# Six instead of three of the 28 products of a unit in an inner seven-product form, with every engine's order taken from a table: pooled attention and a snake-activated two-layer network on one Trainium2 core

## The chip, the cores and the metric

The kernel runs on one core of a Trainium2 chip. The metric is the device time of one execution in microseconds. The kernel before took 906.76 us (median of three runs, 905.39 to 907.78).

The engines are named as in the profile: PE (TensorE matmul) and PEld (its weight loads), DVE (VectorE), ACT (ScalarE), POOL (GpSimd), SP (SyncE, which issues most DMAs). Each works through its own list of instructions in order and waits on semaphores for the others.

## The reference

All tensors are float32. Attention runs over 8 batches of 8 heads with 576 queries of 64 dimensions; keys and values are first averaged over groups of 8 rows, so each head has 72 of them. The result, as 4608 tokens of 512, goes through a network of two matrices with a "snake" activation.

```python
k_p = k.reshape(B, H, Sp, 8, D).mean(axis=3)
v_p = v.reshape(B, H, Sp, 8, D).mean(axis=3)
scores = scale * np.matmul(q, k_p.transpose(0, 1, 3, 2))
attn = softmax(scores)                     # over the 72 keys
x = np.matmul(attn, v_p)                   # 4608 tokens x 512
h = x @ w_in                               # 512 x 2048
g = h + np.sin(alpha * h) ** 2 / (alpha + 1e-9)
out = g @ w_out                            # 2048 x 512
```

## The kernel before

**Units.** The 4608 tokens are cut into nine units of 512. A unit u has the hidden layer of its tokens (`hidden`, L806) and carries, between its matmuls, the attention of batch u + 1 (`carry`, L1154, puts each piece of it into one of 28 slots). Ahead of unit 0 stands `first_batch`, which loads everything, pools the first batch and computes its attention. Units 7 and 8 carry no attention; at the end of unit 8 the second layer begins (`outputs`), which goes on alone to the end. The hidden activations g travel through DRAM (`g_bridge`) between the two layers.

**Products.** Both layers use Strassen's algorithm in Winograd's form: a product of 2 x 2 blocks is made of seven block products, numbered 1 to 7, of sums of blocks. In the hidden layer the blocks of w_in and their sums (`self.A`, `combine_w_in`, L675 on POOL) are the stationary operands, and the blocks of x and their sums (`sums_of_x`, L804 on DVE, in the tile `home3`, called bt) the moving ones. A unit has four groups J = 0 to 3, each with the seven products in the order 1, 5, 6, 2, 7, 3, 4, so 28 products in all. A product is four matmuls of 128 x 128 by 256 columns (L834). A group holds four PSUM banks b1, b6, b5, b7; ACT copies a bank into the next one where both need the same partial sum (L810), and makes sines and squares (L984, L991); DVE makes the last additions (L809, L1036); the result g is stored (L1050).

**The inner form.** `inner_product` (L1002) splits one of the 28 products once more in the same way: seven matmuls of 128 columns (L1014) in place of four of 256. It is cut into four steps: `a` multiplies 1 and 5 into a bank of their own (7 or 6), and ACT copies both results, the first into two places of the product's bank (L1018) and the second into a small tile m (L1020); `b` multiplies 6 and 2, and ACT copies one quarter of the bank (L1024); `d` multiplies 7, and DVE adds m (L1029); `e` multiplies 3 and 4. The next step of the same product needs the copy or the addition of the step before, so other matmuls are put in between. In units 1 to 6 three of the 28 products have this form: product 5 in groups 2 and 3 and product 1 in group 3. Their sums of weights are made once, in unit 0, by `inner_w_in` (L769) on POOL (L794) in a tile of the q loads; their sums of x are made once a unit by `inner_x` (L782) on POOL (L794).

**Attention of a batch.** Keys and values are loaded (L121, L140, L145) and pooled by POOL (L131). PE turns the keys (L269), computes scores in two blocks (`two_scores`, L308, 32 and 40 matmuls); DVE takes the maximum and subtracts (L331, L332), ACT takes the exponential (L357, with a load of its table and another back to the sine's), DVE sums and inverts (L363, L364), POOL multiplies (L365), DVE turns blocks of 32 (L491 to L501) and 16 DMAs move them (L511); then `all_values` (L600, L613) multiplies with the values, and ACT writes x (L527). The q of a later batch is turned in the same way (L219, L224) and moved by 16 DMAs (L234).

**Order.** The order of instructions on each engine is that of the program's text: `hidden` writes the matmuls of its seven products by hand, with the extras of each slot between them and copies, sines, squares and additions placed one by one, partly a group late (`last_sines`, `finish_before`, `behind_order`). Tiles are taken from pools, and a tile's next use waits for all readers of the last.

Of the kernel before, what the change touches and what calls it, by code (L numbers as in the profile page):

```python
# [19 lines left out]
P = 128  # L20
POOL = 8
# [3 lines left out]

class Kernel:
    def __init__(self, tc, q, k, v, w_in, w_out, alpha, out):
        self.tc, self.nc = tc, tc.nc
# [12 lines left out]
        self.T = self.S // 4  # L56

        self.gd = self.nc.dram_tensor("g_bridge", (2, self.NJ * JW, P, self.B * self.S), F32, kind="Internal").ap()

    def home(self, i, shape):  # L60

        return (self.xp if i < 2 else self.xq).tile(shape, F32, name=f"home{i}")
# [15 lines left out]
    def q_tile(self, i):  # L78

        return self.qp.tile([P, 5 * self.H * self.D], F32, name=f"q{int(i)}")  # L80
# [35 lines left out]
    def load_k(self, b, e):  # L116
# [3 lines left out]
        t = self.kvp.tile([P, 2048], F32, name="kvin")[:NP * m, 0:3 * POOL * D]  # L120
        self.nc.sync.dma_start(out=t, in_=self.k[b, NP * e:NP * e + NP].rearrange("h (p x) d -> (h p) (x d)", x=3 * POOL))  # L121
        if b not in self.kp:
            self.kp[b] = self.ap.tile([NP * m, 3, 2, D], F32, name="kp")
# [9 lines left out]
    def load_v(self, b):  # L133

        nc, D, H = self.nc, self.D, self.H
        vm, vz = self.vp[b] = self.ap.tile([P, H // 2, D], F32, name="vm", bufs=2), self.ap.tile([P, H // 2, D], F32, name="vz", bufs=2)
        t = self.kvp.tile([P, 2048], F32, name="kvin")[:].rearrange("p (h x) -> p h x", h=4)
        x = self.kvp.tile([P, POOL * D], F32, name="vr", bufs=1)[:]
# [40 lines left out]
    def load_v_rows(self, b, main, rest):  # L179
# [6 lines left out]
        self.vp[b] = self.ap.tile([P, self.H // 2, self.D], F32, name="vm", bufs=2), self.ap.tile([P, self.H // 2, self.D], F32, name="vz", bufs=2)  # L186
# [19 lines left out]
    def turn_q(self, b, part):  # L206
# [8 lines left out]
        if part == 0:  # L215
            for e in range(2):
# [3 lines left out]
                if e == 0:  # L220
                    self.finish_before()
# [17 lines left out]
    def new_tr(self):  # L239
        return self.ap.tile([P, 20 * 5 * 32], F32, name="tr")[:]  # L240
# [8 lines left out]
    def attention(self, b):  # L249
# [44 lines left out]
        def two_scores(j):  # L294

            x = (self.turn + 1) % 5
# [22 lines left out]
        def shifts(i, m, ps):  # L319
# [6 lines left out]
            for z, o in zip(ps, y):  # L326
                w = list(z.shape)[:-1]
                mx = self.sm.tile([P, 12], F32, name="mx2")[:, 0:m * (1 + i % 2)]
# [15 lines left out]
        def shift(i, e, ps):  # L344

            n = rows[i]
            mx = self.sm.tile([P, NP], F32, name="mx")
# [11 lines left out]
        def norm(i):  # L359

            n = E(i).shape[1]
            sm = self.sm.tile([P, 12], F32, name="sm2")[:, 0:n]
# [4 lines left out]
        def new_a():  # L367
            self.aM = self.ap.tile([P, 4, 736], F32, name="aM")
# [71 lines left out]
        def norm_rest():  # L440

            n = 64
            sm = self.sm.tile([P, H], F32, name="sm")
# [146 lines left out]
        def all_values():  # L590
# [16 lines left out]
            nc.scalar.copy(out=self.sm.tile([P, 1], F32, name="order")[:], in_=rest[:, 1, 0:1])  # L607
# [7 lines left out]
            self.behind_order()  # L615
            self.behind_order = lambda: None
# [152 lines left out]
    def inner_w_in(self):  # L769

        w = self.q_tile(0)[:]
        at = 0
        for p, J0 in ((5, 2), (1, 3)):
            n = self.NJ - J0
            A = self.A[p][:].rearrange("p k (J j m) -> p k J j m", j=2, m=P)[:, :, J0:]
            L = lambda i, j: A[:, j, :, i]
            s1, s2, s3, s4 = (w[:, at + i * n * P:at + (i + 1) * n * P].rearrange("p (J m) -> p J m", m=P) for i in range(4))
            at += 4 * n * P
            self.sums(((s1, L(1, 0), L(1, 1), OP.add), (s2, s1, L(0, 0), OP.subtract), (s3, L(0, 0), L(1, 0), OP.subtract), (s4, L(0, 1), s2, OP.subtract)))
            self.W2[p] = J0, {1: L(0, 0), 2: L(0, 1), 3: s4, 4: L(1, 1), 5: s1, 6: s2, 7: s3}  # L780

    def inner_x(self, u):  # L782

        for p, x, out in ((5, self.bt[u][:, 0], self.last[:, 0:4 * P]),
                          (1, self.xT[u][:, 0:2, 0:TH], self.ex[:, 5].rearrange("p h x -> p (h x)")[:, 0:4 * P])):
# [20 lines left out]
    def hidden(self, u, extra):  # L806
# [4 lines left out]
        sin, square, early = self.sin, self.square, lambda G: G.J == (0 if G.u else 1)  # L811
        two = 0 < u < self.B - 1

        def begin(J):

            b1, b6, b5, b7 = (self.bank([P, JW, TH]) for _ in range(4))
            new = lambda n, **kw: self.hp.tile([P, 2, JW, 2, TH], F32, name=n, **kw)
            G = SimpleNamespace(u=u, J=J, b1=b1, b5=b5, b6=b6, b7=b7, g=new("h"), s=self.s,
                                p5=None, i1=None, i5=None, early=J == (0 if u else 1))
            if two and J > 1:  # L820
                G.i5 = self.inner_product(G, 5, b5, 7)
# [757 lines left out]
```

## Time and profile before

| what | value |
|---|---|
| three runs | 905.39, 906.76, 907.78 us |
| profiled execution: span from first to last instruction | 902.6 us (the trace gives no other time for it; the median lies 4.2 us above) |
| granted clock of TensorE | 1.000 |
| busy: POOL, DMA traffic | 210.5 us; 141.13 MB, 156 GB/s in the mean |
| first batch | 0 to 20 us, PE busy 20.0 |
| unit 0 | 20 to 86.45 us |
| units 1 to 6 | 86.45 to 416.8 us, 55.0 to 55.15 us each |
| unit 7 and most of unit 8 | 416.8 to 513 us, PE without idle time |
| second layer | to the end; 56 steps of seven products |

How to read it: a matmul's row in the trace has a modelled end, and matmuls overlap in the array, so the time that one costs is the distance of its start from the next one's. Every float32 matmul stands in the trace as two records, so a plain product is 8 records and an inner one 14. A "busy" PE can still hide holes of up to some 0.15 us in front of a record. PEld loads the weights of the next matmul beside PE; a wait for a semaphore is often booked there.

### The profile page before, as it was taken

To read this page: it belongs to the slowest core of one execution; us is meant where nothing else is said; L and a number is where in the kernel's file an instruction comes from. 1 tells how busy PE (TensorE), PEld (TensorE's weight loads), DVE (VectorE), ACT (ScalarE), POOL (GpSimd) and SP (SyncE) were. 2 spreads that over 40 slices of the span, in tenths; PEclk is the share of its full clock that TensorE was granted. 3 is DMA by queue.
4 is the path that set the end of the run, shared out by engine and by line. 5 is a ranking of instruction groups with operands and counts; after the bars stand their busy time and mean duration, and the time that the engine had idled before them with its cause. 6 is when DMAs were issued, how large, how long until landed. Compare 5 with 4: busy or idle time off the path is not lost.

```text
span 902.6 us, 17941 instructions
## 1 busy us (share of the span) xinstructions
PE 895.0 (99%) x7014; PEld 815.8 (90%) x7014; DVE 677.4 (75%) x1011; ACT 448.3 (50%) x1070; POOL 210.5 (23%) x216
## 2 busy tenths in 40 slices
PE   8999999999999999999999999999999999999998
PEld 5787888888888888888888999999999999999997
DVE  7685766768577685764458799979798888889895
ACT  5696776877768778687976611111111111111111
POOL 4788552824438253430000000000000000000000
PEclk9999999999999999999999999999999999999999
DMA  9965867759586595648216346261618162534401
GB/s 261 245 200 158 220 163 202 196 167 251 139 213 186 177 230 143 176 146 293 93 72 227 102 141 199 59 194 38 224 27 230 33 197 67 172 92 127 137 15 40
DMA packets 128747, 141.13 MB, mean 156 GB/s; under 512 B 46920, under 2 KB 95704, under 8 KB 128664
## 3 DMA queue, kind: packets, MB, share of 16 engines
q1 hardware_dynamic: 125880, 137.88, 53.2%
q10 hardware_dynamic: 2784, 2.11, 0.9%
q8 instruction: 56, 0.92, 0.4%
q14 instruction: 27, 0.22, 0.1%
HBM read 75.37 MB, written 47.19 MB: 136 GB/s over the span
## 4 chain that ended last, share of the span: by engine, by line
PE 91%; DMA 3%; DVE 2%; POOL 2%; SPq 1%; issue 0%; ACT 0%; DVEq 0%; POOLq 0%
PE PS L834 42%; PE PS L1312 41%; PE PS L1014 3%; PE PS L308 2%; PE PS L600 2%; DMA a<-in_moe_w_in_dram 2%; DMA kvin<-in_v_dram 1%; SPq L669 1%; PE PS L613 1%; DVE x L1267 1%; DMA h<-in_k_dram 1%; POOL kvin L131 0%; POOL as L675 0%; DVE s L1267 0%; POOL ex L365 0%
## 5 line engine op out<-in xcount | busy, mean ns | idle before, releaser
L834 PE MATMUL PS<-home,a 128*128 128x256 f32 x1104 | 257.9, 381 | 0.7 <-ACT home L527 0.5
L834 PEld LDWEIGHTS PS<-home,a 128*128 128x128 f32 x1104 | 205.2, 190 | 34.1 <-issue 5.0
L834 PE MATMUL PS<-home,as 128*128 128x256 f32 x768 | 183.0, 382 | 0.0
L834 PEld LDWEIGHTS PS<-home,as 128*128 128x128 f32 x768 | 141.6, 190 | 19.8 <-ACT PS L810 1.2
L1312 PE MATMUL PS<-s,wb 128*128 128x144 f32 x896 | 119.1, 286 | 0.0
L1362 POOL TENSOR_TENSOR cc<-cc,cb 128x576 f32<-128x576 f32 x1 | 2.0, 1976 | 501.8 <-DVE cb L1267 501.8
L1312 PEld LDWEIGHTS PS<-s,wb 128*128 128x128 f32 x896 | 113.7, 190 | 0.1
L991 ACT ACTIVATE s<-s,c 128x256 f32<-128x256 f32 (+1 forms) x228 | 113.5, 564 | 0.0
L809 DVE TENSOR_TENSOR h<-PS,p 128x512 f32<-128x512 f32 x72 | 49.2, 683 | 64.2 <-PE PS L834 36.3
L131 POOL TENSOR_TENSOR kvin<-kvin 96x768 f32<-96x768 f32 (+3 forms) x42 | 71.6, 1705 | 69.5 <-DMA kvin<-in_v_dram 67.9
L1440 ACT COPY PS<-PS 128x144 f32<-128x144 f32 x56 | 14.7, 263 | 145.0 <-PE PS L1312 135.5
L984 ACT ACTIVATE s<-h,al 128x256 f32<-128x256 f32 x144 | 65.6, 510 | 39.4 <-DVE h L809 39.3
L1312 PE MATMUL PS<-r,wb 128*128 128x144 f32 x512 | 73.3, 286 | 0.3 <-DVE r L1267 0.3
L1312 PE MATMUL PS<-s,a 128*128 128x144 f32 x512 | 73.2, 286 | 0.0
L1036 DVE TENSOR_TENSOR h<-PS,s 128x512 f32<-128x512 f32 x36 | 24.7, 687 | 59.8 <-ACT s L991 59.8
L984 ACT ACTIVATE s<-PS,al 128x256 f32<-128x256 f32 x144 | 60.1, 470 | 18.6 <-PE PS L834 17.7
L1312 PEld LDWEIGHTS PS<-r,wb 128*128 128x128 f32 x512 | 67.1, 190 | 0.5 <-DVE r L1267 0.5
L1312 PEld LDWEIGHTS PS<-s,a 128*128 128x128 f32 x512 | 67.1, 190 | 0.0
L810 ACT COPY PS<-PS 128x512 f32<-128x512 f32 x72 | 41.5, 576 | 35.0 <-PE PS L834 30.4
L1460 ACT COPY PS<-PS 128x144 f32<-128x144 f32 x56 | 14.7, 263 | 88.1 <-PE PS L1312 88.1
L1312 PE MATMUL PS<-s,we 128*128 128x144 f32 x384 | 54.9, 286 | 0.0
L1312 PE MATMUL PS<-x,wb 128*128 128x144 f32 x384 | 54.9, 286 | 0.0
(215 smaller groups left out, 1407.7 us busy)
## 6 DMA issues: line engine op xcount, KB each, us to landing
g_bridge<-h SPq DMA_DIRECT2D x72, 512.0 KB
r<-g_bridge SPq DMA_DIRECT2D x31, 1152.0 KB
out_dram<-o SPq DMA_DIRECT2D x122, 72.0 KB
kvin<-in_k_dram SPq DMA_DIRECT2D x14, 576.0 KB
q<-in_q_dram SPq DMA_DIRECT2D x7, 1024.0 KB
kvin<-in_v_dram SPq DMA_DIRECT2D x14, 512.0 KB
aM<-tr SPq DMA_DIRECT2D x54, 92.0 KB
aM<-tr SPq DMA_DIRECT2D x54, 88.0 KB
```

Source lines behind the costliest of these rows:

```text
L131: self.nc.gpsimd.tensor_tensor(out=t[..., 0:w] if w > D else out, in0=t[..., 0:w], in1=t[..., w:2 * w], op=OP.add)
L308: nc.tensor.matmul(ps[e][r0 + r:r0 + r + q.shape[-1], h, :], q[s], kb[s, hp, :], start=True, stop=True)
L600: nc.tensor.matmul(o[r:r + 64], w, x, start=start and i < 2, stop=False, skip_group_check=True)
L809: add = lambda o, x, y: nc.vector.tensor_tensor(out=o, in0=x, in1=y, op=OP.add)
L810: copy = lambda o, x: nc.scalar.copy(out=o, in_=x)
L834: nc.tensor.matmul(ps[:, jj, :], self.A[p][:, kk, f * P:(f + 1) * P], x[:, kk, :], start=(start and n == 0), stop=(kk == 1), skip_group_ch ...
L984: self.nc.scalar.activation(out=G.s[:, i, jj, j, :], in_=src[:, jj], func=AF.Sin, scale=self.al[:, f:f + 1])
L991: self.nc.scalar.activation(out=x, in_=x, func=AF.Square, scale=self.c[:, f:f + 1])
L1014: nc.tensor.matmul(o, W[m][:, G.J - J0], X[m], start=start and n == 0, stop=True, skip_group_check=True)
L1036: add = lambda o, x, y: self.nc.vector.tensor_tensor(out=o, in0=x, in1=y, op=OP.add)
L1312: nc.tensor.matmul(out, W[:, J // 2, J % 2, :], A[:, J, :], start=(start and J == 0), stop=(J == self.NJ - 1), skip_group_check=True)
L1440: nc.scalar.copy(out=x1[:, 0, :], in_=x0[:, 1, :])
```

## The change

Three things change together.

1. In units 1 to 6 the groups J = 1, 2 and 3 have both product 1 and product 5 in the inner form: six of 28 products.
2. `hidden` is written anew. In those groups product 1 of the next group is made step by step between the matmuls of products 7, 3 and 4, and product 5 between those of 6 and 2. In group 0 of these units product 5 stands behind product 7, and the two score blocks stand in slot 1 and in the middle of product 2, where they stood in slots 3 and 5.
3. A class `Order` stands between the kernel and the engines. It records each instruction with the regions that it reads and writes, gives each a key (part, unit, label, number), sorts each engine's list by a place from the table `PLAN`, keeps PE in the order of the text, and then emits them all so that none comes ahead of what it depends on. Tiles of one name become one lasting tile (or a ring of two or three), so that a later use waits for the regions that it touches.

Beside that, `inner_w_in` makes 24 sums of 128 columns instead of eight (four of 256, four of 128), the x sums of product 1 get a tile of their own, two squares of half size are joined in groups that had them apart, and the loads of g for the second layer stand behind a step's work instead of ahead of it, in another order.

The core of the diff:

```diff
+    def flush(self):
+        self.edges()
+        lines = {e: [t for t in self.tasks if t.eng == e] for e in self.ENG.values()}
+        for e, x in lines.items():
+            for n, t in enumerate(x):
+                t.at = n if e == "PE" else t.unit * UNIT.get(t.key[0][0], 0) + self.plan.get(t.key, 0)
+            x.sort(key=lambda t: t.at)
...
+            x = min(ready, key=lambda x: (x[0].eng != "PE", x[0].at))
+            t = x.pop(0)
+            t.f(*t.a, **t.k)
...
-        for p, J0 in ((5, 2), (1, 3)):
...
+        for J in range(self.J0, self.NJ):
+            for p in (5, 1):
...
+            extras()
+            product(G, 6, G.b6, (0, 1))
+            if two:
+                G.i5.a()
+            product(G, 6, G.b6, (2, 3))
+            copy(G.b7[:], G.b6[:])
+            if two:
+                G.i5.b()
+            extras()
+            product(G, 2, G.b1, (0, 1))
+            if two:
+                G.i5.d()
+            if J == 0:
+                for f in extra["mid"]:
                     f()
+            product(G, 2, G.b1, (2, 3))
+            if two:
+                G.i5.e()
...
+            product(G, 7, G.b7, (0, 1))
+            if N and not late:
+                N.i1.a()
+            product(G, 7, G.b7, (2, 3))
+            if late:
+                N.i1.a()
+                product(G, 5, G.b5, start=True)
+                copy(G.p5[:], G.b5[:])
+            add(G.g[:, 1, :, 1], G.b7[:], G.p5[:])
+            self.sin(G, 1, 1, G.g[:, 1, :, 1])
+            extras()
+            if N:
+                N.i1.b()
+            product(G, 3, G.b6, (0, 1))
+            if N:
+                N.i1.d()
+            product(G, 3, G.b6, (2, 3))
...
+            if N:
+                N.i1.e()
+            product(G, 4, G.b7)
...
-                if n == 3 and u + 1 < self.B:
-                    self.load_g(u + 1, ("r11", "r12", "r22"))
-                if n == 5 and u + 1 < self.B:
-                    self.load_g(u + 1, ("r21",))
...
+            if st and u + 1 < self.B:
+                self.load_g(u + 1, {3: ("r11", "r22"), 4: ("r12",), 5: ("r21",)}.get(n, ()))
```

On the engines' lists this makes 72 matmuls of 256 columns fewer and 126 of 128 columns more on PE, 54 more copies of the inner form on ACT with 24 squares of 256 columns fewer and 12 of 512 more, 18 more additions on DVE, and 16 more operations on POOL. The number of DMAs is the same. In unit 0, POOL's list has one of the new weight sums in front of the sums of w_in's second group, nine more among the sums of keys and values, and the other 14 behind; SP's list has single loads and stores of several kinds in turn where it had them kind by kind.

## The prediction, made before the changed kernel ran

> **What bounds the kernel now.** I read the page's first two parts, then the busy times by stage, then TensorE's instructions in order of time, then the chain of work that ended last.
>
> ```profile
> PE 895.0 (99%) x7014; PEld 815.8 (90%) x7014; DVE 677.4 (75%) x1011; ACT 448.3 (50%) x1070; POOL 210.5 (23%) x216
> PEclk9999999999999999999999999999999999999999
> ```
>
> TensorE (PE) is busy for 99% of the span at its full granted clock, so time is won only by giving PE less to do or by closing the small holes that a "busy" row, whose ends are modelled, hides. By stage:
>
> ```profile
> 20.00:84.70 64.70, 64.48 (x531) 51.66 (x532) 42.74 (x75) 46.68 (x100) 54.45 (x54) 1.00 0.77 211
> ...
> 540.00:902.00 362.00, 358.31 (x2925) 358.09 (x2924) 306.59 (x409) 62.30 (x199) 1.98 (x1) 1.00 0.41 117
> ```
>
> Columns: stretch, its length, then busy time (and count) of PE, PEld, DVE, ACT, POOL, then clock, DMA share, GB/s. Unit 0 (first row) has GpSimd (POOL) busy for 54.45 of 64.70 us, more than anywhere else; units 1 to 6 (next row, one of them) keep ACT at three quarters; in the output stage only PE and DVE matter.
>
> ```profile
> 141.50:196.60 55.10, 55.10 (x447) 47.22 (x447) 38.17 (x63) 41.19 (x96) 25.56 (x25) 1.00 0.71 193
> ```
>
> What one record costs PE is the distance of starts, not the record's length:
>
> ```profile
> 118.48 2.76 PE L834 MATMUL PS<-home,a 128*128 128x256 f32 x12
> 121.08 0.38 PE L1014 MATMUL PS<-home,q 128*128 128x128 f32 x2
> 121.30 0.39 PE L1014 MATMUL PS<-last,as 128*128 128x128 f32 x2
> 121.52 1.03 PE L834 MATMUL PS<-home,a 128*128 128x256 f32 x4
> 122.39 0.38 PE L1014 MATMUL PS<-home,a 128*128 128x128 f32 x2
> ```
>
> Twelve 256-column records take 121.08 - 118.48 = 2.60 us, 0.216 each; four 128-column records take 121.52 - 121.08 = 0.44, 0.111 each. Every f32 matmul is two records. The last chain confirms that PE sets the end:
>
> ```profile
> 537.40 360.92 PE PS L1312 x2944
> ```
>
> From 537.40 to the end PE never waits (360.92 / 2944 = 0.1226 a record). Nothing is to be won there; one hole of about 0.5 us lies just before, at 535 to 537, behind a DVE sum of 2.48 us.
>
> **The change, part by part.**
>
> *Products.* In units 1 to 6, 25 of 28 products are plain (4 matmuls of 256 columns: 8 x 0.216 = 1.727 us) and 3 are in the inner form (7 matmuls of 128: 14 x 0.1115 = 1.561, a few ns more for the changes of shape). After the change 6 are inner; the built order agrees (72 matmuls of 256 columns fewer, 126 of 128 more). So 18 products win 1.727 - 1.57 = 0.16 each: -2.9 us. This is on PE, which sets the end, and is nearly sure.
> The Trainium skill (TensorE: Matmul & The Clock Gate, "Wait — 56ns, not 53.3ns?") says that a warm matmul takes its columns at 2.4 GHz plus a fixed 2.5 ns or so, a reason against splitting. By it, as an estimate, two f32 passes a record would give 215.8 ns, as the rows do, and 109.2 ns where the rows give 111; the step would be -3.5 instead of -2.9 us. The rows decide.
>
> *Holes in units 1 to 6.* The period is (416.8 - 86.45) / 6 = 55.06 us. By rows PE needs 43.2 (plain) + 4.7 (inner) + 2.8 (scores, L308) + 3.4 (values, L600 and L613) + 0.25 (keys, L269) = 54.3. So 0.75 us a unit are holes. About half is the restart after a change of shape and stays. The rest are waits: the first scores wait 0.38 us a unit for the DVE add that finishes the unit before (PEld L308 behind DVE L1036, 2.3 us in 6 times), and products wait for an ACT copy (PEld L834 behind ACT L810, 2.3 us in 12 times). The new order moves that add and gives each bank copy its place; bounds are 0 and -0.4 a unit. I take -0.17: -1.0 us in six units.
>
> *New hand-offs.* Each inner product adds two ACT copies after its first pair, one after its second and one DVE add before its last:
>
> ```profile
> L1018 ACT COPY PS<-PS 128x256 f32<-128x256 f32 x18 | 6.7, 375 | 5.0 <-DVE PS L1029 4.9
> L1020 ACT COPY m<-PS 128x128 f32<-128x128 f32 x18 | 5.0, 276 | 0.0
> L1024 ACT COPY PS<-PS 128x128 f32<-128x128 f32 x18 | 4.5, 250 | 11.9 <-PE PS L1014 11.9
> ```
>
> The last two numbers ahead of the idle time are busy us and mean ns. Three more products a unit: 3 x (375 + 276 + 250) = 2.7 us of ACT, less 0.6 for squares that are joined (24 of 510 ns fewer, 12 of 714 ns more, over six units): 41.2 becomes 43.3 of some 54.4 us. DVE gets 3 x 433 ns (L1029): 38.2 becomes 39.5. Both lie beside PE. What could reach PE is the wait: between the steps of an inner product the new code mostly puts two plain matmuls, 0.86 us. From the start of a pair's last record, cover is 0.11 + 0.86 = 0.97 us and need is 0.27 (the record) + 0.375 (the copy) = 0.65, or 0.70 with DVE's 433. If a sine of 0.47 to 0.51 us stands ahead on ACT, or an add of 0.68 on DVE, the step is 0.2 to 0.4 late. The rows above show such a spacing today (pairs at 121.08 and 122.39 with four records of 0.216 between) and no lateness. I take 0; the ends are 0 and 0.2 late for a third of the 108 hand-offs, +7 us.
>
> *The earlier scores.* The two score blocks move forward in the unit, with 2.6 us of PE between them instead of 3.65. DVE has to empty the first block in that: 4 operations of 0.45 and 2 of 0.75, 3.3 us, of which the first 0.4 lie beside the block itself and the second block's late banks give another 0.55. It just fits if DVE does nothing else, and the order of DVE holds those six together. Cost 0, at most 0.3 a unit. The 16 moves of q (0.63 us each on SP) end earlier with it in units 2 to 6; at the start of unit 1 they end about when the second block wants them: +0.3, bounds 0 and +1.5.
>
> *Unit 0 on GpSimd.* The weights of the inner form become 24 operations of 128 columns instead of 8 longer ones:
>
> ```profile
> L794 POOL TENSOR_TENSOR ex<-home,ex 128x128 f32<-128x128 f32 x12 | 11.4, 946 | 0.5
> L794 POOL TENSOR_TENSOR last<-home 128x128 f32<-128x128 f32 x12 | 10.7, 888 | 88.9 <-DVE home L804 88.9
> ...
> L794 POOL TENSOR_TENSOR ex<-home 128x128 f32<-128x128 f32 x12 | 5.4, 454 | 0.0
> ```
>
> That is 24 x 0.45 = 10.9 to 24 x 0.95 = 22.7 us for today's 5.2 (79.73 to 84.4 by time). Ten of them stand ahead of the last sums of k, whose reader on PE comes at 84.44. In the new order one weight sum stands in front of the combinations of w_in and writes where the first score block of unit 0 reads, which ends at 36.9 on PE; GpSimd is idle from 32.6 until then (4.3 us), where it works today. From 37.0 on I add the rows up: 12 combinations of 1.27 (15.2), norms 5.1, sums of v 5.2 + 2.1, of k 7.6, small ones 2.9, ten weight sums at 0.55 (5.5), some 2.0 between them: 45.6 us, to 82.6. PE's demands come at 77.2 (product 7 of the last group), 79.0 (values) and 84.4 (k): 1 to 2 us of margin by these means. I take +0.3, ends 0 and +5.
>
> *The rest.* Later loads of g (a product or two of 0.98 us later, needed 20 us on) and the new order of the output stage: PE waits for nothing there today, DVE at 85% has little room; 0, ends -0.5 (the hole at 535) and +1.
>
> Sum: -2.9 - 1.0 + 0.3 + 0.3 = -3.3 us. The profiled execution has a span of 902.6; the three timed runs have a median of 906.76 (905.39 to 907.78), 4.2 more, for what lies around the span and for its being a good run. The sum is a difference and goes on the median: **903.5 us**. About 0.3% (2.7 us) is what a measurement of this kernel can tell from no change, so the forecast lies just beyond it.
>
> **Rivals.**
> 1. *Hand-offs late.* ACT and DVE work in order at 79% and 73%; if 18 of the 108 hand-offs are 0.18 late, the gain of 3.3 is gone; with 36 the time is 903.5 + 6.5 = 910.0, with 15 it is 906.2. For it: the spacing is mostly 0.86 now, where two of today's three products have 1.7 to 3.5 us at their first step. Against it: today's tight one loses nothing, and in the built order the copies stand ahead of the second of each pair of sines. Chance 0.20.
> 2. *GpSimd sets unit 0 (slower).* Place: POOL between 37 and 84 us. Price: ten weight sums at 0.89 instead of 0.45 (+4.4), sums of k and v at their long ends (+2.4), less about 1.9 of margin: +4.9, of which 0.3 is in the sum: 908.1 us. It decides from 3.6 us of lateness, that is when the sums ahead of k take 51 us instead of 45.6. For it: one shape takes 454 and 946 ns here, short at 79.7 to 84.4 us, where DVE is busy 1.32 of 4.67 us, mostly long at 87.4 to 93.3, where it is busy 4.96 of 5.90. Against: the rows of k, v and norms, which are most of the sum, were taken beside that same DVE. Chance 0.20. The Trainium skill (SBUF — State Buffer, "Terms") says that DVE and GpSimd arbitrate for one port pair and the loser stands for the whole instruction; the two windows agree with it. By it, as an estimate with DVE busy for two thirds of unit 0, most of the ten sums would stand at the long end, and this rival would be about as likely as the forecast.
> 3. *Another form than told.* If fewer than 6 products were inner, each would give 0.16 x 6 = 0.96 us back (906.4 with none new); the built order speaks against it. Chance 0.03.
>
> **How the numbers follow.** Forecast 0.57, of which 0.50 lies under 904.0 and 0.07 above; rival 1: 0.14 within 0.3%, 0.06 slower; rival 2: 0.12 and 0.08; rival 3: 0.03 within. So faster 0.50, same 0.36, slower 0.14. The low end, 900.5, takes all holes' bounds (-2.4) and the hole at 535 (-0.5) with the 2.9, nothing lost at the start (901.0), and 0.5 for the spread of the runs; the high end, 907.9, reaches into both rivals.
>
> **What would show it.** Right: units 1 to 6 start 54.3 to 54.6 us apart, 0.111 us per 128-column record, score blocks without the wait for L1036, unit 1 starting at 86 to 87 us, output stage as long as before. Wrong: holes of 0.1 to 0.4 between inner steps that end with an ACT copy or a DVE add (rival 1), or PE waiting for POOL at 77 to 85 us and unit 1 starting after 89 (rival 2). A change of time in the output stage would refute the sum's last term.

## The result, and the profile after

The changed kernel takes **909.18 us** (median of six runs, 908.26 to 909.87) against 906.08 for the kernel before on the same chip (six runs, 905.11 to 907.78): ratio 1.0036, 95% interval 1.0025 to 1.0047. It is 3.1 us slower, where 2.6 us faster was forecast, and lies above the range (900.5 to 907.9). In the tables below "+" is slower.

The profiled execution has a span of 907.6 us; the one of the kernel before had 902.6. First the page's own first part and its clock line, then busy time by stage (stretch, its length, busy time and count of PE, PEld, DVE, ACT, POOL, clock, DMA share, GB/s), both of the changed kernel:

```profile
PE 894.9 (99%) x7122; PEld 813.5 (90%) x7122; DVE 661.0 (73%) x1029; ACT 458.2 (50%) x1112; POOL 199.0 (22%) x232
...
PEclk9999999999999999999999999999999999999999
```

```profile
22.40:88.90 66.50, 63.93 (x528) 51.28 (x529) 41.80 (x74) 45.96 (x95) 52.85 (x56) 1.00 0.68 183
144.20:199.10 54.90, 54.90 (x464) 46.97 (x463) 37.41 (x66) 42.42 (x103) 22.79 (x25) 1.00 0.68 193
545.00:907.00 362.00, 358.32 (x2926) 358.11 (x2924) 297.13 (x407) 63.87 (x199) 1.98 (x1) 1.00 0.41 116
```

PE's busy time is the same to 0.1 us with 108 records more, and the clock is full. Unit 0 (first row) has 2.6 us in which PE stands; before it had 0.2. The records themselves cost what was said: in the timeline of PE, four 256-column records take 190.12 - 189.25 = 0.87 us and four of 128 columns 189.25 - 188.81 = 0.44.

```profile
188.81 0.38 PE L156 MATMUL PS<-ex,q 128*128 128x128 f32 x2
189.03 0.39 PE L156 MATMUL PS<-home,as 128*128 128x128 f32 x2
189.25 1.03 PE L156 MATMUL PS<-home,a 128*128 128x256 f32 x4
190.12 0.41 PE L156 MATMUL PS<-ex,q 128*128 128x128 f32 x2
```

PE's waits in the changed kernel (engine, tile, line <- releaser: us in total, times, longest) are where to begin. All instructions that the class records show the line that emits them, L156, so one goes by tiles:

```profile
PE PS L156 <- DVE h L156: 2.1, 2, 1.2
PE PS L156 <- DMA q<-in_q_dram: 1.7, 1, 1.7
...
PE PS L156 <- POOL as L156: 0.9, 1, 0.9
...
PE PS L156 <- ACT PS L156: 0.5, 1, 0.5
```

The rest is bookkeeping by landmarks that both traces have: the first 256-column record (first product of unit 0), the turn of the keys (96x96) in each unit, the first and last 128x144 record of the second layer. From unit 1's end on the keys stand one product (1.73 us) later in the changed kernel's unit, which is taken out.

| stretch | before | after | difference |
|---|---|---|---|
| start to the first product of unit 0 | 19.98 | 22.38 | +2.40 |
| to the keys in unit 0 | 13.68 | 13.73 | +0.05 |
| to the keys at the end of unit 0 | 50.78 | 52.85 | +2.07 |
| unit 1 | 55.09 | 55.25 | +0.16 |
| units 2 to 5 | 220.44 | 219.63 | -0.81 |
| unit 6 to the end of unit 8 | 148.30 | 149.98 | +1.68 |
| output stage | 389.75 | 389.22 | -0.53 |
| its end | 4.61 | 4.60 | -0.01 |
| span | 902.63 | 907.64 | +5.01 |

A single profile is a weak witness at its start: this one began unit 0 at 22.4 us, where the six other profiles with the same start (experiments 2, 3, 4, 12 and the first ones of 9 and 10) begin it at 20.5 to 21.8. Units 1 on repeat to a few hundredths between profiles of the same code. Unit 0 takes 52.85 us wherever its code is that of the changed kernel, except once, 50.94 (experiment 12). The kernel before is no steadier there: its unit 0 took 50.78 in this profile and 50.22 in those of experiments 7 and 8, so the loss in unit 0 is 2.1 to 2.6 us. Outside the span there is another difference: time less span is 1.79 us in the runs of the kernel before and 2.25 in those of the changed one, +0.46.

### The profile page after: what moved, and what is told of

The parts are those of the page before. It is cut to its first block, busy times and chain, and to the rows that moved or that the text cites. A ratio compares the mean times of both kernels' runs of the same rounds, so it can differ in the third digit from the quotient of the medians.

```text
span 907.6 us, 18285 instructions
## 1 busy us (share of the span) xinstructions
PE 894.9 (99%) x7122; PEld 813.5 (90%) x7122; DVE 661.0 (73%) x1029; ACT 458.2 (50%) x1112; POOL 199.0 (22%) x232
## 4 chain that ended last, share of the span: by engine, by line
PE 95%; DMA 2%; ACT 1%; POOL 1%; DVE 1%; issue 0%; SPq 0%; DVEq 0%; POOLq 0%; ACTq 0%
PE PS L156 95%; DMA q<-in_q_dram 1%; ACT s L156 1%; POOL as L156 1%; DMA h<-in_k_dram 1%; DVE h L156 0%; SPq L156 0%; POOL a L156 0%; ACT L156 0%; ACT PS L156 0%; DVE mx L156 0%; DVE ex L156 0%; ACT ex L156 0%; DVE o L156 0%; DVE cc L156 0%
## 5 line engine op out<-in xcount | busy, mean ns | idle before, releaser
L156 ACT COPY PS<-PS 128x144 f32<-128x144 f32 (+4 forms) x312 | 115.8, 372 | 297.3 <-PE PS L156 285.4
L156 PE MATMUL PS<-home,a 128*128 128x256 f32 (+1 forms) x1080 | 252.0, 374 | 2.5 <-DVE h L156 2.1
L156 PEld LDWEIGHTS PS<-home,a 128*128 128x128 f32 x1080 | 195.6, 190 | 31.2 <-issue 4.5
L156 PE MATMUL PS<-home,as 128*128 128x256 f32 (+1 forms) x792 | 187.5, 372 | 1.4 <-POOL as L156 0.9
L156 PEld LDWEIGHTS PS<-home,as 128*128 128x128 f32 x792 | 143.0, 190 | 19.9 <-ACT PS L156 1.8
L156 PE MATMUL PS<-s,wb 128*128 128x144 f32 x896 | 119.1, 286 | 0.0
L156 ACT ACTIVATE s<-s,c 128x256 f32<-128x256 f32 (+1 forms) x216 | 117.6, 582 | 0.9 <-DVE h L156 0.7
L156 PEld LDWEIGHTS PS<-s,wb 128*128 128x128 f32 x896 | 113.7, 190 | 0.1
L156 POOL TENSOR_TENSOR cc<-cc,cb 128x576 f32<-128x576 f32 x1 | 2.0, 1978 | 498.5 <-DVE cb L156 498.5
L156 ACT ACTIVATE s<-h,al 128x256 f32<-128x256 f32 x144 | 70.8, 507 | 29.1 <-DVE h L156 28.7
L156 DVE TENSOR_TENSOR h<-PS,p 128x512 f32<-128x512 f32 x72 | 49.2, 684 | 47.8 <-PE PS L156 24.8
L156 POOL TENSOR_TENSOR kvin<-kvin 96x768 f32<-96x768 f32 (+3 forms) x42 | 69.9, 1665 | 41.3 <-DMA kvin<-in_k_dram 40.3
L156 ACT ACTIVATE s<-PS,al 128x256 f32<-128x256 f32 x144 | 63.8, 474 | 20.8 <-PE PS L156 20.4
L156 PE MATMUL PS<-r,wb 128*128 128x144 f32 x512 | 73.2, 286 | 0.0
L156 PE MATMUL PS<-s,a 128*128 128x144 f32 x512 | 73.2, 286 | 0.0
L156 DVE TENSOR_TENSOR h<-PS,s 128x512 f32<-128x512 f32 x72 | 48.8, 678 | 30.8 <-ACT s L156 30.8
L156 PEld LDWEIGHTS PS<-r,wb 128*128 128x128 f32 x512 | 67.1, 190 | 0.1
L156 PEld LDWEIGHTS PS<-s,a 128*128 128x128 f32 x512 | 67.0, 190 | 0.0
L156 POOL TENSOR_TENSOR ex<-ex,sm 128x576 f32<-128x576 f32 (+1 forms) x28 | 36.4, 1301 | 113.9 <-DVE sm L156 108.2
L156 PE MATMUL PS<-s,we 128*128 128x144 f32 x384 | 54.9, 286 | 0.0
L156 PE MATMUL PS<-x,wb 128*128 128x144 f32 x384 | 54.9, 286 | 0.0
L156 DVE TENSOR_TENSOR PS<-PS,m 128x256 f32<-128x256 f32 x36 | 15.6, 433 | 51.6 <-PE PS L156 49.4
```

The source lines that it names most:

```text
L156: t.f(*t.a, **t.k)
```

## The experiments

All ratios are to the kernel before, whose runs were taken on the same chip in the same series; 0.001 is 0.9 us. The table's lists are edited at one or two entries; `[27]` is entry 27 of a key.

**1. The start.** The trace's 1.7 us wait is for a load of q. SyncE issues it at 8.82 us, behind a load of w_in; before, it was issued at 6.99.

```profile
14.72 0.66 PE L156 MATMUL PS<-twos,home 128*128 128x64 f32 x4
17.09 0.66 PE L156 MATMUL PS<-ident,q 128*128 128x128 f32 x4 [1.71 <-DMA q<-in_q_dram]
```

```diff
-a.: ... [27] 391 [28] 477
+a.: ... [27] 298 [28] 300
```

> The changed kernel with one difference: SyncE issues the load of the q heads that the first turns of q need (the fourth load of q) and the second half load of v ahead of the first load of w_in, as the kernel before did. Theory A (places in the table lose the time): TensorE's wait of 1.7 us at 14.7 us for that load goes, everything behind it moves forward by as much; keys of unit 0 start at 34.4 instead of 36.1 us, and the time is 1.7 us under the changed kernel's 909.2, so +1.4 us or +0.15% over the kernel before. Rival B (the wait only moves): w_in then comes late, TensorE waits for it at 20 us, and the time stays at +3.1 us. Rival C (the start's loss was the spread of transfers in one run): the wait is gone or not by chance, time as the changed kernel's.

Measured: 1.0027 (1.0016 to 1.0039), 0.8 us better than the changed kernel; the wait is gone and unit 0 begins at 20.06. But ScalarE then waited for a later load of q and PE lost 0.9 us behind it before the keys. So the named wait went, as A said, and another came, though not the one for w_in that B named. The 0.8 by the clock is inside the intervals of the two ratios. Part of the 1.7 was C: the later kernels with this place unmended wait 0.4 to 1.5 us for that load and begin unit 0 at 20.5 to 21.8; those with it mended begin at 20.1 to 20.4. The means, with the changed kernel's own 22.4 among the late ones, differ by 1.0 us, which I take for what this place costs.

**2. The store at the end of unit 7.** A hole of 1.0 us at 479.4 us, by the distance of starts, ends with an addition into h. In the changed kernel:

```profile
479.91 0.69 DVE L156 TENSOR_TENSOR h<-PS,p 128x512 f32<-128x512 f32 x1 [1.73 <-PE PS L156]
...
480.64 0.91 ACT L156 ACTIVATE s<-h,al 128x256 f32<-128x256 f32 x2 [2.60 <-DVE h L156]
480.66 1.38 PEld L156 LDWEIGHTS PS<-home,a 128*128 128x128 f32 x7 [1.24 <-DVE h L156]
480.66 1.56 PE L156 MATMUL PS<-home,a 128*128 128x256 f32 x6 [0.84 <-DVE h L156]
```

The row of DVE names PE as its releaser. But the addition also waits for the store that reads its buffer, and SyncE's list shows that store late (changed kernel):

```profile
465.64 9.55 SPq L156 DMA_DIRECT2D g_bridge<-h  x4
475.29 5.09 SPq L156 DMA_DIRECT2D r<-g_bridge  x3
```

Four stores stand in one row, the first at 465.6 and the other three from 473.4. The table has one half of the first buffer's store behind both of the second's, which exist only at 473.4.

```diff
-7.: ... [158] 43592 [159] 43595 ... [210] 43594 [211] 43593
+7.: ... [158] 43592 [159] 43593 ... [210] 43595 [211] 43594
```

> The changed kernel with one difference: at the end of unit 7 SyncE issues both halves of the store of h's first buffer ahead of the two stores of its other buffer; the table had one half behind them, so that it waited for the last group of the unit. Theory A: the first addition of unit 8 into that buffer no longer waits for the late store (1.73 us of idle DVE), TensorE's hole of 1.0 us at 479.4 us goes, and the time is 1.0 us under the changed kernel's 909.2: +2.1 us over the kernel before. Rival B: the addition waits for TensorE, as the profile's row names it, and the hole of 1.0 stays: +3.1 us.

Measured: 1.0021 (1.0011 to 1.0031), 1.4 us better; unit 6 to the end of unit 8 takes 148.62 instead of 149.98. In this kernel's trace the same addition waits for nothing, so the named releaser was the wrong one and A holds:

```profile
475.13 1.28 DVE L156 TENSOR_TENSOR we<-wb,we 128x512 f32<-128x512 f32 x2
476.42 0.69 DVE L156 TENSOR_TENSOR h<-PS,p 128x512 f32<-128x512 f32 x1
```

**3. Unit 0, by its waits.** Two places were read off the trace; holes are given by the distance of starts, so that they are a little longer than the waits in brackets. PE stands 1.0 us at 47.7, put down to GpSimd; but I read that operand as GpSimd's sum that was done at 43.75, and ScalarE's bank copy, too, ended just before PE's start, in its list behind two sines, a copy and a square:

```profile
47.36 0.72 ACT L156 ACTIVATE s<-s,c 128x512 f32<-128x512 f32 x1
...
47.39 1.28 POOL L156 TENSOR_TENSOR as<-a,as 128x512 f32<-128x512 f32 x1
...
47.99 0.58 ACT L156 COPY PS<-PS 128x512 f32<-128x512 f32 x1
...
48.71 1.10 PE L156 MATMUL PS<-home,as 128*128 128x256 f32 x4 [0.89 <-POOL as L156]
```

And 1.4 us at 57 to 58.7, behind a DVE addition that took 3.38 us instead of 1.2 to 1.5 and made all of DVE's list late. It began 0.05 us behind one of GpSimd:

```profile
51.78 2.35 POOL L156 TENSOR_TENSOR kvin<-kvin 128x1024 f32<-128x1024 f32 x1
51.83 3.38 DVE L156 TENSOR_TENSOR h<-h,s 128x1024 f32<-128x1024 f32 x1
...
54.09 1.43 POOL L156 TENSOR_TENSOR q<-as 128x128 f32<-128x128 f32 x1
```

```diff
-0.: ... [49] 4148 ... [56] 2830 ... [80] 4155
+0.: ... [49] 4156 ... [56] 2227 ... [80] 4151.5
```

> The changed kernel with three places of unit 0 changed: ScalarE makes the bank copy for product 6 of group 1 ahead of two sines, a q copy and a square; VectorE adds product 5 (h<-PS,p) ahead of the sum of exponentials, and the addition over 1024 columns behind it. Theory A: the holes of 1.0 us (47.4) and 1.4 us (57.1 to 58.7) on TensorE go, and much of that at 64: -2 to -2.5 us, so +0.6 to +1.1 us over the kernel before. Rival B: VectorE meets GpSimd's long rows at another place, the 1024-column addition takes 3.4 instead of 1.3 us there too, and the lateness comes back before unit 1: +2.5 to +3.1 us.

Measured: 1.0037 (1.0023 to 1.0051), no gain by the clock. In the trace both holes are gone, and units 0 and 1 are 1.0 us shorter; a new hole of 1.2 us stands before the second score block, and the one near 64 us grew from 0.5 to 0.8. That settles the releaser of the first hole: here the same product starts at 46.36, behind the moved bank copy (done at 46.14), while GpSimd is still at the sums of 45.43 to 47.93. A on the two holes; B on the time but not by its path, since the addition over 1024 columns took 1.21 us at its new place: a mended wait let the next one through.

**4. The value products.** They take 3.82 us a unit instead of 3.42. A one-column copy that frees a bank for them stands behind a bank copy and a square on ScalarE (changed kernel):

```profile
192.92 0.19 PEld L156 LDWEIGHTS PS<-aM,vm 64*64 64x64 f32 x6 [0.24 <-ACT p L156]
...
193.15 0.62 ACT L156 COPY PS<-PS 128x512 f32<-128x512 f32 x1
...
193.66 0.19 ACT L156 COPY order<-PS 128x1 f32<-128x1 f32 x1
...
193.90 0.19 PEld L156 LDWEIGHTS PS<-aM,vm 64*64 64x64 f32 x4 [0.37 <-ACT order L156]
```

```diff
-u.all_values : ... [10] 8612
+u.all_values : ... [10] 8609.5
```

> The changed kernel with one place changed, in units 1 to 6 alike: ScalarE's one-column copy that the value products wait for stands directly behind the copy of product 5, ahead of a square and a bank copy. Theory A: the value products (3.82 us a unit in the changed kernel, 3.42 before) lose 0.2 to 0.35 us a unit, units 54.6 us apart instead of 54.9: -1.2 to -2.1 us, +1.0 to +1.9 us over the kernel before. Rival B: the bank copy that now comes 0.2 us later is what TensorE waits for next, and units stay 54.9 apart: +3.1 us.

Measured: 1.0031 (1.0019 to 1.0043); units 54.79 apart instead of 54.90. A in direction, but 0.11 us a unit where 0.2 to 0.35 were said: the other wait of this place, for the copy p, stayed. By the clock 0.5 us is not told from nothing.

**5. All of it, with the waits that followed.**

```diff
-0.load_v : ... [4] 1289      0.q_t : ... [19] 2849 [24] 2852
+0.load_v : ... [4] 1700      0.q_t : ... [19] 2235 [24] 2238
-0.: ... [108] 4436           u.: ... [216] 8609
+0.: ... [108] 4401           u.: ... [216] 8607.5
```

> The changed kernel with all four mended places together and the waits that came up behind three of them mended too: one load of v goes behind the q loads in the start (one run had ScalarE wait for that q), the q copies of unit 0 go ahead of a sine and two squares (the score block waited for them, 1.24 us), the bank copy of group 2 in unit 0 goes ahead of a sine and two squares (0.84 us), and in units 1 to 6 the copy of product 5 goes ahead of a sine (0.25 us a unit). Theory A (the places in the table lose the time, and each lost wait can be given its time back): from the changed kernel's +3.1 us, less 0.8 (start, as measured alone), 1.35 (store), 1.0 + 2.1 (unit 0), 0.7 + 0.6 to 1.5 (value products): -3.5 to -4.3 us under the kernel before, units 2 to 6 54.5 to 54.7 apart. Rival B (a wait that goes lets the next one through): only what the four gave alone, 0.8 + 1.35 + 1.0 + 0.7 = 3.85, -0.7 us.

Measured: 1.0005 (0.9996 to 1.0014), by 1.1 us worse than B, which gave 0.7 under the kernel before, and far from A. Start, store and value products keep their gains (units 54.74 apart), but unit 0 still takes 52.69: waits of 1.8 us before the score block, now behind a VectorE addition that waits for ScalarE's squares, and 0.9 behind 64.7. Two holes that move together when one is mended made me look for a cause further up the lists.

**6. No table at all.**

```diff
-                t.at = n if e == "PE" else t.unit * UNIT.get(t.key[0][0], 0) + self.plan.get(t.key, 0)
+                t.at = n
```

> The changed kernel with the table left out: every engine keeps the order of the text, with the same products on TensorE in the same order. Theory A (the table's misplaced entries are a few; most of it helps, since the text of the new form puts each bank copy behind the sines and squares of the group before): slower than the changed kernel by 5 us or more, with waits of 0.2 to 0.6 us on ScalarE copies in every group of units 1 to 6; period over 55.5 us. Rival B (ordering by the table is itself what loses): 903 to 906 us, period 54.3 to 54.6.

Measured: 1.246 (1.2401 to 1.2518), 1130 us; 87.4 to 88.8 us a unit. A, and far beyond its 5 us. Lines of this kernel's page and the two largest of PE's waits:

```profile
PE 983.4 (87%) x7122; PEld 863.4 (76%) x7122; DVE 679.1 (60%) x1029; ACT 463.1 (41%) x1112; POOL 203.3 (18%) x232
...
PEclk9989889898888888888988999999999999999999
```

```profile
PE PS L156 <- ACT PS L156: 95.4, 56, 3.4
PE PS L156 <- DVE ex L156: 29.9, 24, 2.8
```

The text of the new form is no order to run in, and the table is worth some 220 us against it. So the table as a whole does not lose the time; which entries do, experiments 1 to 5, 9 and 10 show. The granted clock is lower too, 0.933 in the mean, and in this trace it is 0.5 in stretches of 3.41 us or twice that. The Trainium skill (TensorE: Matmul & The Clock Gate, "HAM oscillation — how this bites in real kernels") says that pauses of more than about 3.4 us bring TensorE back to half rate. This run shows it behind shorter ones:

```profile
112.19:115.60 3.41, 1.12 (x33) 1.00 1.00 329
115.60:119.01 3.41, 3.06 (x51) 0.50 1.06 225
```

Columns: stretch, its length, PE's busy time and count, clock, DMA share, GB/s. PE's pauses in the first row and across its end are 1.39, 0.52 and 0.73 us, and the clock is halved in the next. Each half-rate stretch of this trace begins behind 3.41 us in which PE was busy for 1.36 us or less.

**7. One inner product fewer in the kernel before.**

```diff
-            if two and J > 1:
+            if two and J > 2:
...
-                    if not (two and J == 1):
+                    if True:
```

> The kernel before with two instead of three of a unit's 28 products in the inner form (product 5 of group 2 plain). Theory A: the inner form's price holds in any order, 1.76 us for a plain product and 1.59 for an inner one by the distances of starts: 6 products more in plain form, +1.0 us. Rival B: what the inner form saves is lost in its hand-offs: 0 or below.

Measured: 0.9988 (0.9978 to 0.9998) by the clock, but units 55.16 apart in its trace instead of 55.06, so 0.6 us slower in six units. The two disagree, and the clock's difference is of the size of the spread: the kernel before ran from 904.2 to 908.5 us in this series. The trace gives 0.10 us for a product in this order, less than the 0.167 expected: the eight plain records more add 1.65 us and not 1.73, so some 0.08 us of small holes went with the inner product, whose 14 records take 1.56. By the clock this stays open.

**8. The late load of q in the kernel before.**

```diff
             self.nc.sync.dma_start(out=self.v_rows[0][:, h:h + 4].rearrange("p h t d -> p h (t d)"),
                                    in_=self.v[b, h:h + 4, 0:4 * P, :].rearrange("h (p t) d -> p h (t d)", t=4))
+            if h == 0:
+                self.load_w_in_part(0, (1,))
```

> The kernel before with one difference in the start: SyncE issues the first load of w_in between the two half loads of v, so that the q load of heads 6 and 7 is issued behind it, as in the changed kernel. Theory A: TensorE waits 0.4 to 1.7 us for that load at 13 to 15 us, and the time is +0.4 to +1.7 us. Rival B (the load lands in time in either order, and the changed kernel's start was a chance of its profiled run): no wait, 0.

Measured: 1.0007 (0.9996 to 1.0018): not told from nothing by the clock. Its trace waits 0.3 us for that load, and unit 0 begins at 21.39 instead of 19.98, of which 0.6 is a longer wait for keys, earlier, that the load has nothing to do with, and some 0.5 has no wait to its name. So by the profiles the late load costs 0.3 us here and up to 1.7 in the changed kernel.

**9. What lay under unit 0.** ScalarE in the changed kernel stands 2.84 us, up to 44.41, for an addition of VectorE ahead of the squares of group 0, of which the first ran at 35.9 us before. The kernel before has the same wait, 2.83 us, but it ends at 40.44: counted from the first product of unit 0, 20.5 us there and 22.0 here. VectorE's list in the changed kernel:

```profile
40.71 0.74 DVE L156 TENSOR_TENSOR ex<-PS,mx 128x576 f32<-128x576 f32 x1
41.37 0.80 DVE L156 TENSOR_SCALAR t<-t 128x16 f32<-128x16 f32 x1
42.09 0.44 DVE L156 TENSOR_REDUCE mx<-PS 128x4 f32<-128x288 f32 x1
42.46 0.44 DVE L156 TENSOR_TENSOR ex<-PS,mx 128x288 f32<-128x288 f32 x1
42.82 0.96 DVE L156 TENSOR_TENSOR c<-c,t 128x16 f32<-128x16 f32 x1
43.70 0.68 DVE L156 TENSOR_TENSOR h<-PS,p 128x512 f32<-128x512 f32 x1
```

Two of the rows that refine the factor c of the squares (16 columns each) stand among the scores and take 0.80 and 0.96 us ahead of the addition. Before, all four of these rows ran at 22.0 to 25.3 us. The first attempt put them ahead of the sums of x, which was a mistake:

```diff
-a.: ... [220] 2152 [221] 2177 [222] 2201 [223] 2226
+a.: ... [220] 2080 [221] 2081 [222] 2082 [223] 2083
```

> The changed kernel with one difference: the four 16-column rows of VectorE that refine the factor c of the squares stand ahead of the additions of x in unit 0, where VectorE is idle for 3.6 us, and not among the score rows at 34.8 to 43.8 us. Theory A (one cause in unit 0: no square can run before c is done, so ScalarE has its squares behind 43.8 us where the kernel before had the first at 35.9, and the late copies and additions of the next groups follow from it): ScalarE and VectorE get ahead by 1.5 us or more, the holes of TensorE at 47.4, 58.7 and 64 us (1.0, 1.4, 0.5) shrink together to under 1, and units 0 and 1 last 2 us less: +0.8 to +1.3 us over the kernel before. Rival B (the order of ScalarE and VectorE in each group makes its own hole): unit 0 no more than 0.5 us shorter, +2.6 us or more.

Measured: 1.0050 (1.0038 to 1.0062), slower. But the distances say what happened: unit 0 from keys to keys takes 50.52 instead of 52.85, as A said, and the stretch in front of it 15.59 instead of 13.73, because PE now waits for the row behind the four:

```profile
26.56 0.46 PE L156 MATMUL PS<-ident,as 64*128 64x64 f32 x4 [1.78 <-DVE home L156]
```

The same entries went into a version with start, store and value products mended.

> The changed kernel with the start, the store of unit 7 and the value products mended as in the run with all places, and unit 0 by the early refinement of c alone, without the six moves of that run. Theory A: the run with all places was at the kernel before (+0.4 us) and had 2.6 us of holes left in unit 0; with the one cause gone 1.5 to 2 us of them go, -1.1 to -1.6 us under the kernel before. Rival B (waits only move): within 0.5 us of the kernel before.

Measured: 1.0019 (1.0007 to 1.0030), 1.7 us over the kernel before and so worse than both A and B; the stretch in front of the keys takes 15.9 us, as in the run before.

**10. The four rows where nobody waits.** VectorE has 3.6 us of idle time behind the copy into aM.

```diff
-a.: ... [220] 2152 [221] 2177 [222] 2201 [223] 2226
+a.: ... [220] 2137 [221] 2138 [222] 2139 [223] 2140
```

> The changed kernel with the four rows that refine c placed behind the copy into aM, where VectorE is idle for 3.6 us, and not ahead of the additions of x as in the run before (there TensorE waited 1.9 us for the row behind them, and what units 0 and 1 won, 2.3 us, was spent in front of them). Theory A (early c wins the 2.3 us wherever the rows delay nobody): start to keys of unit 0 as in the changed kernel (13.7 us from the first product), unit 0 to keys of unit 1 50.5 us instead of 52.85: -2.3 us, +0.8 us over the kernel before. Rival B (the rows' own time, some 2.7 us beside GpSimd, is paid by TensorE wherever they stand): +3 us.

Measured: 1.0008 (0.9996 to 1.0021), by the ratios +0.7 us where the changed kernel has +3.3; 13.76 us to the keys and 50.53 from there. The size is A's, but the path was not the one given: c itself was not awaited. The squares stand behind ScalarE's wait for VectorE's addition, and the rows had held up that addition by 0.80 + 0.96 us; ScalarE, in order, made everything behind it late. Now the wait ends at 41.32, again 20.4 us behind the first product. And the pair of long additions of experiment 3 (at 51.8 us there) came out the other way round: h<-h,s starts first here, at 49.45, and takes 1.99 us. How much of the gain is that, experiment 12 shows.

> The same place for c together with the mended start, store and value products. Theory A: the changed kernel's +3.1 us less 2.3 (c) and 0.5 (unit 1), 0.8 (start), 1.35 (store) and 0.85 (value products): -2 to -2.7 us under the kernel before, a ratio of 0.997 to 0.998, and most of what six products save is there. Rival B: a wait somewhere in unit 0 takes it up, within 0.5 us of the kernel before.

Measured: **0.9984 (0.9974 to 0.9995)**, 903.67 us against 905.39: faster than both kernels, by a little less than A said. From the keys of unit 0 its trace has 49.74 (unit 0), 54.73 (unit 1), 218.97 (2 to 5), 148.45 and 389.22 us. PE's waits are down to

```profile
PE PS L156 <- DVE full L179: 1.1, 1, 1.1
PE PS L156 <- ACT home L156: 0.5, 1, 0.5
PE PS L156 <- DVE home L156: 0.4, 1, 0.4
PE PS L156 <- ACT q L156: 0.2, 1, 0.2
PE PS L156 <- ACT h L156: 0.2, 1, 0.2
```

**11. Four inner products in that version.**

```diff
-        self.J0 = 1
+        self.J0 = 2
...
```

The lines left out give each instruction that stays its old place in the table and keep group 1 in the order of the other groups.

> The best version so far (start, store, value products and c mended) with four instead of six inner products in units 1 to 6: products 1 and 5 of group 1 are plain, their six ScalarE copies, two VectorE additions and GpSimd's eight weight sums are left out, and every other instruction keeps its place in the table. Theory A (0.167 us a product, by the distances of starts): units 0.33 us further apart (55.06 instead of 54.73), +2.0 us against the best version, so 0 to +0.5 us against the kernel before. Rival B (the hand-offs take back what the form saves): units no more than 0.1 us further apart, -1.0 to -1.7 us against the kernel before, as the best version.

Measured: 1.0058 (1.0043 to 1.0074), units 55.76 to 56.07 apart. B's 0.1 us is out. But +1.03 us a unit is three times what A said; 0.69 of it are new holes in group 1 (0.23 at one place, 0.03 to 0.10 at six), where the entries for six products no longer fit. What is left, 0.34, is A's price, but the run does not show it apart from the holes. So a table made for one set of products cannot be used to price another.

**12. The 0.46 us outside the span.**

```diff
+                if t.key[0].startswith("p7."):
+                    t.at = 1000000 + n
```

> The changed kernel with the engines' orders in the last eighth of the output stage as in the text. If the 0.46 us outside the span come from the end of the program, time less span is 1.8 us here; if from its head or from elsewhere, 2.25 as in the changed kernel. TensorE's time in the output stage stays 389.2 us (within 0.5).

Measured: 1.0042 (1.0030 to 1.0055); time less span 2.24 us in the mean of eight runs (2.19 to 2.28), output stage 389.22. It is not the end. With four products it was 2.44 and without the table 1.80; where it comes from stays open.

But the profile of this kernel, whose order up to unit 7 is that of the changed one, has 50.94 us in unit 0 instead of 52.85; PE stands neither at 57 to 58.7 nor near 64. Nothing had been changed there. The two additions of experiment 3 had fallen the other way round (all lines stand two further down, L158):

```profile
50.01 1.46 DVE L158 TENSOR_TENSOR h<-h,s 128x1024 f32<-128x1024 f32 x1
...
50.35 3.35 POOL L158 TENSOR_TENSOR kvin<-kvin 128x1024 f32<-128x1024 f32 x1
```

VectorE comes first by 0.34 us and takes 1.46 instead of 3.38, and the one that stands is GpSimd, which has room. In the profiles of the changed kernel and of experiments 1, 2 and 4 GpSimd came first by 0.05 to 0.07 us, and unit 0 took 52.83 to 52.85. So by this one profile up to 1.9 of its 2.1 us hang on a race of some hundredths of a microsecond. In the five kernels of experiments 9 to 11 with the four rows moved, VectorE came first in every profile, by 0.7 us or more. So these rows cost some 0.4 us by themselves (50.94 - 50.53), and beyond that they set who comes first.

## Why the prediction was wrong

The sum was -3.3 us, of which -2.5 of its -2.9 for the products came. The step that failed is the price of the new order: the sum prices what the change adds and a few waits that it removes, and the rows and DMA issues that were there before and now stand elsewhere in their engines' lists have no term (the value products, SyncE's issues) or one for the wrong engine (unit 0, +0.3). In their place the runs show +2.4 at the value products, +2.1 in unit 0, +1.4 at a store and about +1.0 at a load of q.

- **Products, -2.9.** Right in kind. A unit has 24 records of 256 columns fewer (-5.20 us by distances of starts) and 42 of 128 more (+4.78): -0.42 a unit with hand-offs, -2.5 in six.
- **New hand-offs, 0.** Nearly right, and inside the -0.42: holes of 0.10 and 0.07 at the first inner product of a unit. Rival 1 came once: unit 1 lasts 0.35 us longer than the others at one step of an inner product, where PE waits for VectorE's addition of m (below). That is what the 0.35 is, and not the scores.
- **Holes in units 1 to 6, -1.0.** Right in size: PE's small holes shrank by 0.19 a unit, -1.1, of which 0.10 at the scores, though their weights still wait 0.33 us behind other rows of VectorE. But the sum lacked a term: the value products, which wait for ScalarE's copies, cost +0.40 a unit, +2.4. Moving two copies took 0.17 of it back (54.73 apart in experiment 10); what holds the rest is not shown.
- **The earlier scores, +0.3.** Did not come: the scores take 2.62 us of PE in unit 1 as in the units behind it, and 2.72 before. What unit 1 loses is here, in the changed kernel:

```profile
117.15 0.43 DVE L156 TENSOR_TENSOR PS<-PS,m 128x256 f32<-128x256 f32 x1 [0.51 <-ACT s L156]
...
117.64 0.30 PEld L156 LDWEIGHTS PS<-home,q 128*128 128x128 f32 x2 [0.48 <-DVE PS L156]
```

  It is the same in the profiles of experiments 9 (first run) and 12, where unit 0 is short (50.52 and 50.94, then 55.26 and 55.28 for unit 1), and gone in those of experiments 3 and 10 (54.91 and 54.73). So it does not hang on the length of unit 0; which entry decides it stays open.
- **Unit 0 on GpSimd, +0.3.** Here the path was the wrong one: 2.1 us, and not by GpSimd's added work. The weight sums took 0.45 us each but one of 1.43, so they were at the short end, and PE did not wait for them at 77 to 85 us; GpSimd even stood 4.2 us as foreseen. I looked at the engine that got the most new operations, and the loss was on VectorE and ScalarE, whose lists only changed their order: the four rows of c, moved by 13 to 19 us into the busiest stretch, made VectorE late enough that GpSimd came first at the pair of long additions in four of five profiles. Rival 2 gave nearly the right time (908.1) by the wrong mechanism, which is luck.
- **The rest, 0 with ends -0.5 and +1.** The lower end was right: -0.53 in the output stage, where VectorE's long sum now stands ahead of the step's additions. The upper end was too small by far, since it was taken for the loads of g and the output stage alone. Two moves of SyncE's list were not priced: the load of q (about +1.0 in the mean of the profiles) and the half store in unit 7 (+1.4).
- **Outside the span, +0.46**, was not thought of, and its cause stays open.

In sum: units 1 to 6 -0.83 (products -2.5, named waits -1.1, value products +2.4, unit 1 +0.35), unit 0 +2.1 (by the profile whose unit 0 took 50.78), the half store +1.4, the other of units 7 and 8 +0.5, the start +1.0, the output stage -0.53, outside the span +0.46. That is +4.1, beside 3.1 measured. The difference lies, as far as it can be placed, in which runs were profiled: the one of the kernel before (902.63 + 1.79 = 904.4 us) is 1.7 us shorter than its median of 906.08, and no profile shows where its other runs lose that. Where the table's entries are mended the kernel is at 903.67, and the forecast had been 903.5. That they agree is luck: it was forecast of another order, and against the 905.39 of its own series the mended kernel wins 1.7 us and not 3.3.

## What to carry to other kernels

A change that moves every engine's order is not priced by what it adds: go through each engine's list for rows that moved past others, the small ones and the DMA issues first, and ask who stands behind them. When a wait is mended, look at distances between landmarks and not only at that wait, for the next one may stand right behind it; two holes that move together can have a cause further up the list, as here. An order made for one set of operations has to be made anew for another: with four inner products the table for six lost 0.69 us a unit in new holes.

## What the runs showed of the hardware

- VectorE and GpSimd stopped each other for whole instructions here, and whoever started first went on. Behind a GpSimd addition by 0.05 us, VectorE's addition over 1024 columns took 3.38 us; ahead of it by 0.34, it took 1.46, and GpSimd's took 3.35 instead of 2.35 (both shown above). The next GpSimd row, 128 x 128, took 1.43 in the one case and 0.46 in the other. A 16-column row of VectorE took 0.11 to 0.26 us at its shortest and 0.60 to 1.74 where GpSimd held it up; the two of experiment 9 end at 42.17 and 43.78, each 0.02 or 0.03 us behind a GpSimd row. Rows of VectorE that read PSUM were not stretched: the addition at 43.70 us of experiment 9 took its usual 0.68 us while GpSimd was at sums from 43.70 to 46.21. This agrees with the Trainium skill (SBUF — State Buffer, "SBUF: two separate sides"), which tells of an exclusive lock between the two engines.
- A releaser named in a row can be wrong when an instruction waits for several: in experiment 2 it named PE and was a store, in experiment 3 GpSimd and was ScalarE.
- The same order's start differs by 2 us between profiles and unit 0 by 1.9, while the units behind it repeat to a few hundredths. A single profiled span is no measure of 0.3%.
